# First MLP of a fused attention and two-MLP kernel: Strassen products in two token tiles where there were five, with another order of products and PSUM banks

## The chip, the cores and the metric

One core of one Trainium2 chip runs the kernel. The metric is device time of one execution in microseconds; a lower time is better. The profile is of one further execution of the same program.

## The reference, cut to what matters

```python
def reference(...):                       # 8 batches, 8 heads, 576 tokens, 64 per head
    q_s = softmax(q, axis=-1); k_s = softmax(k, axis=2)          # linear attention
    kv = einsum('bhsd,bhse->bhde', k_s, v)
    x = einsum('bhsd,bhde->bhse', q_s, kv) -> (4608 tokens, 512)
    xn = x / sqrt(mean(x * x) + 1e-6) * rms_g                    # first MLP, 512 -> 1536 -> 512
    x = (silu(xn @ w_gate) * (xn @ w_val)) @ w_out
    h = x @ w_in                                                 # second MLP, 512 -> 2048 -> 512
    return (h * sigmoid(1.702 * h)) @ w_out2
```

All results are float32; the weights arrive as float64, and the kernel decodes them into float32 on the chip.

## The kernel before

The 4608 tokens are cut into nine tiles of 512 (tile 0 to tile 8, `NTILE`). The first stage runs tile by tile: in tile j it computes the first MLP of tile j, and beside it the attention of tile j + 1 (four units of two heads each, nine steps a unit, `unit_steps`, L346), the norm of tile j + 1 (`norm_steps`, L483) and a share of the decoding of the second MLP's weights. Attention is finished in tile 6, since a batch has 576 tokens and its eighth batch covers tiles 7 and 8. Then the second stage computes the second MLP; the change does not touch it.

Every float32 product on TensorE is made of three passes of a rounded and a rest part (`PASSES`): high x high, high x rest, rest x high. So each operand needs a high half (a copy on ScalarE) and a low half (a subtraction on VectorE or GpSimd).

**Direct tiles** (0, 1, 2 and 8). The MLP's hidden dimension is cut into 12 blocks n. In three slots a block (36 slots a tile) TensorE makes the gate product of a block (`hidden`, 4 x 3 matmuls of 512 columns, PSUM tag "gv"), the value product, and then the output products of the block before (`out1_parts`, 12 matmuls into four "acc" banks). ScalarE takes silu of the gate, VectorE multiplies by the value (L1252) and splits the result in two halves (`split_u`). After the value product of the last block, the normalised tokens of the next tile are split into four "xs" rooms (`split_x`).

**Strassen tiles** (3 to 7, `by_strassen`, `FIRST, LAST = 3, NTILE - 2`). Two hidden blocks and both halves of the tokens and of the model dimension make a pair m, six pairs a tile. A pair takes seven products of quarter size in the order (1, 6, 2, 7, 5, 4, 3), each 2 x 2 x 3 matmuls of 256 columns, gate and value side by side in one bank. This is a step; a tile has 42 steps. Products 1, 6 and 5 open a bank of tag "gv", of which there are two; 2 adds to the bank of 1, 7 and 4 to that of 6, and 3 to that of 5. VectorE adds the banks to the partial sums (L870) and multiplies silu by value (L835, one step later than silu through the list `late`). After each product TensorE makes up to two output parts of the pair before (3 matmuls each, `PARTS`). Seven of a unit's nine attention steps write PSUM; attention has two banks of tag "att".

The left factors that are sums of weight blocks are made once (`prepare_steps`, L738: GpSimd adds, ScalarE and VectorE split, then stores to DRAM), twelve preparations spread over tiles 1 and 2. They are fetched again by DMA on SyncE's queue into a ring of six half rooms of gate and value weights (`fetch_sum`). The right factors, sums of token blocks, are made by `x_factor` (L790): GpSimd makes the sum (L798), ScalarE the high half, and VectorE or GpSimd the low half, one product at a time, in the last pair of the tile before, or after the last value product where the tile before is direct. Their rooms are four "xs" tiles and three pairs of weight rooms (`ASIDE`).

**What sets the order.** Each engine runs the instructions in the order in which the program lists them; the order is written by hand. `plan[j][slot]` holds the attention, norm and preparation steps of tile j; a Strassen tile maps its 36 slots onto its 42 steps (`plan_by_steps`). Attention steps of the tile behind a Strassen tile are put six slots earlier (`EARLIER`). `store_x2` (L629) empties an accumulator on ScalarE into one of two "ev" rooms and stores it by DMA from ScalarE's queue; in a Strassen tile the stores come as the last parts of the tile before are made, in steps 4, 5, 6 and 6.

PSUM has eight banks: "att" 2, "gv" 2, "acc" 4.

Of the kernel before, what the change touches and what calls it, by code (L numbers as in the profile page):

```python
# [20 lines left out]
def attention_glu_mlp(  # L21
# [58 lines left out]
    NPAIR = NF1 // 2  # L80
    FIRST, LAST = 3, NTILE - 2

# [7 lines left out]
    def f(x):  # L90
        return x.bitcast(F32)
# [241 lines left out]
    def load_v(u):  # L333
# [149 lines left out]
    def norm_steps(j):  # L483
# [59 lines left out]

        def spread():
            if j < 2:
                column_spread()
                return
            for i in range(1, T // P):
                invert(i)
            st["t"] = st["a"]  # L550
# [11 lines left out]

        return squares, total, spread, scale

# [151 lines left out]
    def pack_steps(kind, q):  # L716
# [8 lines left out]
    ITEMS = [  # L725
        (kind, m, p)
        for j in range(FIRST, LAST + 1)
        for m in range(NPAIR)
        for p in ORDER
        if LEFT[p] > 3  # L730
# [58 lines left out]

    def x_factor(j, p):  # L790
        block = [xr[j][:, k // 2 * 2 : k // 2 * 2 + 2, k % 2 * Q : (k % 2 + 1) * Q] for k in range(4)]
        if p in ORDER[:4]:
            w = x_room(8).rearrange("p e (c t) -> p e c t", c=2)
            xs[j, p] = [w[:, :, c] for c in range(2)]
        else:
            i = 2 * ORDER.index(p) - 8
            xs[j, p] = [room1(piece) for piece in ASIDE[i : i + 2]]
        put_op = lambda o, a, b, op: nc.gpsimd.tensor_tensor(o, a, b, op=op)  # L798
        if p in (6, 7, 4):
            x = ap.tile([P, T], F32, tag="sqa", bufs=1, name="xsum").rearrange(  # L800
                "p (c t) -> p c t", c=2
            )
            if p == 4:
                put_op(x, block[3], block[2], ALU.subtract)
                put_op(x, x, block[0], ALU.add)
            else:
                put_op(x, block[2], block[0], ALU.subtract)
                if p == 6:
                    put_op(x, x, block[1], ALU.add)
        elif p == 5:  # L810
            x = block[0]
            put_op(x, x, block[1], ALU.subtract)
        else:
            x = block[RIGHT[p]]
        side = nc.gpsimd if p in (1, 2, 3) else nc.vector
        if p in ORDER[:4]:
            halve(w[:, 0], w[:, 1], x, side)
        else:
            for c, w in enumerate(xs[j, p]):
                halve(w[:, 0], w[:, 1], x[:, c], side)  # L820

# [8 lines left out]
    def strassen_tile(j, plan, parts, aside):  # L830
# [14 lines left out]
        for m in range(NPAIR):  # L845
            d, h, s = {}, {}, {}
            rooms = pools["t"].tile([P, 2, 2, Q], F32, tag="xt", bufs=3, name="h")
            rooms = [rooms[:, 0], rooms[:, 1]]
            for k, p in enumerate(ORDER):
                if p in (1, 6, 5):  # L850
                    d[p] = bank("gv")
                t = d[{1: 1, 2: 1, 6: 6, 7: 6, 4: 6, 5: 5, 3: 5}[p]]
                for i, kind in enumerate("gv"):
                    w = left_factor(kind, m, p)
                    for c in range(2):
                        for n, (a, e) in enumerate(PASSES):
                            nc.tensor.matmul(  # L857
                                t[:, i * Q : (i + 1) * Q],
                                w[:, a, c * P : (c + 1) * P],
                                xs[j, p][c][:, e, :],  # L860
                                start=p in (1, 6, 5) and i == 0 and c == 0 and n == 0,
                                stop=c == 1 and n == 2,
                                skip_group_check=True,
                            )
# [5 lines left out]
                add = lambda o, a: nc.vector.tensor_tensor(o, a, both, op=ALU.add)  # L870
                if p == 1:
                    h["c1"] = rooms.pop(0)
                    nc.scalar.activation(h["c1"], both, AF.Copy)
                elif p == 6:
                    h["u2"] = rooms.pop(0)
                    add(h["u2"], h["c1"])
                elif p == 7:
                    h["u3"] = pools["t"].tile([P, 2, Q], F32, tag="xt", bufs=3, name="h3")
                    add(h["u3"], h["c1"])
                elif p == 2:  # L880
                    s[0] = sp.tile([P, T], F32, tag="s", bufs=2, name="s")
                    later.append(hidden_part(s[0], 1, both))
                else:
                    name, i, o = {5: ("u3", 1, 0), 4: ("c1", 1, 1), 3: ("u2", 0, 0)}[p]
                    add(h[name], h[name])
                    if p == 5:
                        s[1] = sp.tile([P, T], F32, tag="s", bufs=2, name="s")
                    later.append(hidden_part(s[i], o, h[name]))
                    if p != 5:
                        n, half = 2 * m + i, s[i]  # L890
                        later.append(lambda n=n, half=half: split_high(n, half))
                        later.append(
                            lambda n=n, half=half: late["now"].append(lambda: split_low(n, half))
                        )
# [12 lines left out]
                if k == 0 and m:  # L907
                    split_out_weight(2 * m - 2)
                if m == NPAIR - 1:
                    if by_strassen(j + 1):  # L910
                        x_factor(j + 1, p)
                    elif k < NC:
                        split_x(j + 1, k)
            for i in (1, 0):
                parts += out1_parts(j, 2 * m + i)
# [168 lines left out]
    with tc.manual_schedule():  # L1084
# [25 lines left out]
        steps = {u: unit_steps(u, "acc") for u in range(NC)}  # L1110
        squares, total, spread, scale = norm_steps(0)
        for _, u, s in ((x,abs(y),z) for x,y,z in sorted(first)):
# [42 lines left out]

        AT = (-1, 1, 2, 3, 4, 6, 7, 9, 10)
        EARLIER = 6

        for j in range(NTILE):
# [10 lines left out]
            if j + 1 < NTILE:  # L1170
                squares, total, spread, scale = norm_steps(j + 1)
                for c in range(NC):
# [15 lines left out]
        def plan_by_steps(j):  # L1188
            steps1 = [[] for _ in range(NPAIR * 7)]
            for slot in range(SLOTS):  # L1190
                steps1[slot * 7 // 6] += plan[j][slot]
            return lambda k: steps1[k]

# [9 lines left out]
        for j in range(NTILE):  # L1203
            if j == 1:
# [4 lines left out]
                depth.update(stage=1, w32=1)  # L1209
                fetch_next()  # L1210
            if by_strassen(j):
                strassen_tile(j, plan_by_steps(j), parts, aside)
                continue
# [24 lines left out]
            for slot in range(SLOTS):  # L1238
# [5 lines left out]
                elif part == 1:  # L1244
                    tv = hidden(j, weight["v", n])
                    if n == NF1 - 1 and by_strassen(j + 1):
                        for p in ORDER:
                            x_factor(j + 1, p)
# [255 lines left out]
```

## Time and profile before

| | |
|---|---|
| median of 3 runs | 1872.17 us (1871.8 to 1873.7) |
| profiled execution | 1870.15 us |
| its span (first to last instruction) | 1868.3 us |
| first stage, tiles 1 to 8 | 161.87 to 1153.31 us of the span |
| second MLP | 1153.31 us to the end |
| VectorE, ScalarE, GpSimd busy | 1275.2, 863.1, 567.6 us |

Times in the profile are microseconds from the start of the span. PE is TensorE's matmul stream and PEld its weight loads, which overlap it; DVE is VectorE, ACT ScalarE, POOL GpSimd, SP SyncE. A row of the timeline gives start, duration, engine, line, operation, what is written and read, how many were merged, and in brackets the idle time of the engine before it and what ended that. A releaser is inferred: of several things waited for, the last one is named. The clock is the share of TensorE's full speed that was granted.

### The profile page before, as it was taken

Reading aid. Unit: us, or ns where it says so; the run is one execution under the profiler, and the core shown is the slowest. Engines: PE = TensorE matmul, PEld = TensorE weight load, DVE = VectorE, ACT = ScalarE, POOL = GpSimd, SP = SyncE. Lnnn points to the kernel's source line nnn. Section 1 sums busy time; section 2 is a strip of 40 time slices with the busy share of each in tenths; the row PEclk is TensorE's granted clock in tenths of the full one; section 3 lists DMA queues with packets and bytes.
Section 4 is the critical chain, followed back from the end, with each engine's and each line's share of the span. In section 5 each row is a group of like instructions: output and inputs, shape, how many; then the busy total and the mean of one; then the engine's idle time right before and its main releaser. Section 6 shows DMA issues by size and latency. Waiting matters only on the chain.

```text
span 1868.3 us, 29842 instructions
## 1 busy us (share of the span) xinstructions
PE 1728.7 (93%) x11082; PEld 1557.6 (83%) x11082; DVE 1275.2 (68%) x2083; ACT 863.1 (46%) x1491; POOL 567.6 (30%) x506
## 2 busy tenths in 40 slices
PE   6999999968978978978989999999999999999998
PEld 4666777757867867867878888999999999999998
DVE  7997877867766656666645535655565788887776
ACT  6775454446445545444433334544444543333332
POOL 5875665562252242252231152311000510000000
PEclk9999999979989989989999999999999999999999
DMA  6664445446636635645444403455334573444442
GB/s 163 190 183 130 139 132 173 135 139 194 179 108 185 192 114 174 186 123 166 114 135 125 146 23 99 172 179 180 140 133 148 181 249 115 156 136 125 132 129 79
DMA packets 292129, 275.65 MB, mean 148 GB/s; under 512 B 63504, under 2 KB 273424, under 8 KB 291984
## 3 DMA queue, kind: packets, MB, share of 16 engines
q1 hardware_dynamic: 281856, 255.92, 44.8%
q10 hardware_dynamic: 10128, 17.83, 2.6%
q8 instruction: 87, 1.43, 0.3%
q14 instruction: 58, 0.48, 0.1%
HBM read 189.27 MB, written 84.41 MB: 146 GB/s over the span
## 4 chain that ended last, share of the span: by engine, by line
PE 66%; DVE 13%; ACT 8%; DMA 5%; POOL 4%; issue 4%; SPq 0%; ACTq 0%; DVEq 0%; POOLq 0%
PE ps_out L1416 19%; PE ps_in L960 19%; PE ps_gv L581 9%; PE ps_gv L857 8%; PE ps_acc L581 8%; DVE h L870 2%; DMA x<-ev 1%; ACT L396 1%; POOL xsum L798 1%; DVE sqa L542 1%; PE ps_acc L609 1%; DVE qs L402 1%; ACT ke L396 1%; DVE m L358 1%; DVE w L177 1%
## 5 line engine op out<-in xcount | busy, mean ns | idle before, releaser
L960 PE MATMUL ps_in<-xf,w2i 128*128 128x384 f32 x2016 | 350.3, 335 | 0.0
L960 PEld LDWEIGHTS ps_in<-xf,w2i 128*128 128x128 f32 x2016 | 349.9, 188 | 0.3 <-ACT h L972 0.2
L581 PE MATMUL ps_acc<-u,wo 128*128 128x512 f32 x1152 | 307.6, 399 | 0.8 <-ACT ev L637 0.4
L1416 PE MATMUL ps_out<-w2o,uf 128*128 128x256 f32 x2268 | 271.5, 281 | 0.0
L1416 PEld LDWEIGHTS ps_out<-w2o,uf 128*128 128x128 f32 x2268 | 269.6, 188 | 1.1
L186 POOL TENSOR_TENSOR wo<-raw,wo 128x512 fp32r<-128x512 f32 x96 | 130.3, 1358 | 435.1 <-ACT wo L185 369.7
L581 PEld LDWEIGHTS ps_acc<-u,wo 128*128 128x128 f32 x1152 | 205.7, 191 | 37.0 <-ACT ev L637 2.2
L857 PE MATMUL ps_gv<-xs,wg 128*128 128x256 f32 x720 | 119.4, 304 | 44.9 <-DVE h L870 28.4
L857 PEld LDWEIGHTS ps_gv<-xs,wg 128*128 128x128 f32 x720 | 104.8, 204 | 58.9 <-DVE h L870 36.2
L581 PE MATMUL ps_gv<-xs,wg 128*128 128x512 f32 x576 | 147.6, 404 | 4.5 <-DVE xs L573 3.8
L581 PE MATMUL ps_gv<-xs,wv 128*128 128x512 f32 x576 | 143.2, 396 | 1.2 <-POOL wv L186 1.2
L581 PEld LDWEIGHTS ps_gv<-xs,wg 128*128 128x128 f32 x576 | 107.9, 190 | 33.7 <-DVE xs L573 5.0
L870 DVE TENSOR_TENSOR h<-h,ps_gv 128x512 f32<-128x512 f32 x150 | 101.1, 674 | 48.7 <-PE ps_gv L857 45.4
L581 PEld LDWEIGHTS ps_gv<-xs,wv 128*128 128x128 f32 x576 | 106.5, 188 | 25.6 <-POOL wv L186 2.8
L945 ACT ACTIVATE h<-h 128x384 f32<-128x384 f32 x144 | 74.2, 525 | 112.1 <-DVE h L984 87.5
L657 DVE TENSOR_TENSOR raw<-raw 128x256 f32<-128x256 f32 (+1 forms) x236 | 106.6, 494 | 8.7 <-DMA raw<-w2d 6.7
L857 PE MATMUL ps_gv<-xs,wv 128*128 128x256 f32 x720 | 110.9, 292 | 0.0
L984 DVE TENSOR_TENSOR h<-h,ps_in 128x384 f32<-128x384 f32 x144 | 77.7, 552 | 47.7 <-PE ps_in L960 47.5
L834 ACT ACTIVATE s<-h 128x256 f32<-128x256 f32 x90 | 37.6, 418 | 141.8 <-DVE h L870 140.4
L1045 ACT ACTIVATE uf<-raw 128x1792 fp32r<-128x1792 f32 (+2 forms) x38 | 61.6, 1622 | 83.4 <-DVE raw L657 46.1
L857 PEld LDWEIGHTS ps_gv<-xs,wv 128*128 128x128 f32 x720 | 99.9, 200 | 0.0
L182 POOL TENSOR_TENSOR w<-w,stage 128x512 int32<-128x512 int32 x56 | 75.2, 1343 | 62.5 <-PE ps_gv L581 14.9
(202 smaller groups left out, 3018.6 us busy)
## 6 DMA issues: line engine op xcount, KB each, us to landing
u<-h SPq DMA_DIRECT2D x192, 192.0 KB, 1.9
wg<-w1s_g SPq DMA_DIRECT2D x120, 256.0 KB, 4.2
wv<-w1s_v SPq DMA_DIRECT2D x120, 256.0 KB, 4.4
stage<-in_moe_w_out_dram SPq DMA_DIRECT2D x28, 512.0 KB, 3.7
raw<-u SPq DMA_DIRECT2D x24, 512.0 KB, 4.5
x<-ev ACTq DMA_DIRECT2D x34, 256.0 KB, 2.9
stage<-in_moe_w_in_dram SPq DMA_DIRECT2D x16, 512.0 KB, 3.8
w2d<-w SPq DMA_DIRECT2D x32, 256.0 KB, 4.6
```

The costliest lines, as they stand in the source:

```text
L182: return scaled, signed, lambda: nc.gpsimd.tensor_tensor(dst, dst, lo, op=ALU.add)
L186: nc.gpsimd.tensor_tensor(dst[:, 1, :], src, f(dst[:, 0, :]), op=ALU.subtract)
L581: nc.tensor.matmul(t, w(a), x(e), start=first and i == 0, stop=last and i == 2)
L657: engine.tensor_tensor(raw[:, o], raw[:, a], raw[:, b], op=op)
L834: nc.scalar.activation(half, h[:, 0], AF.Silu)
L857: nc.tensor.matmul(t[:, i * Q : (i + 1) * Q], w[:, a, c * P : (c + 1) * P], xs[j, p][c][:, e, :], start=p in (1, 6, 5) and i == 0 and c == ...
L870: add = lambda o, a: nc.vector.tensor_tensor(o, a, both, op=ALU.add)
L945: nc.scalar.activation(dst, src, AF.Gelu_apprx_sigmoid)
L960: nc.tensor.matmul(t, w[:, a, s, c * P : (c + 1) * P], xfac[i, p, c][:, e, :], start=p in (1, 6, 5) and c == 0 and k == 0, stop=c == 1 and ...
L984: nc.vector.tensor_tensor(v, v, t, op=ALU.add)
L1045: nc.scalar.activation(ufac[k][:, 0, piece], uraw[k][:, 1:8][:, piece], AF.Copy)
L1416: nc.tensor.matmul(t[:, i * Q : (i + 1) * Q], u[:, a, LEFT[p] - 1, i * P : (i + 1) * P], w[:, e, m % 2, :], start=m == 0 and i == 0 and n ...
```

## The change

Only tiles 6 and 7 (the seventh and the eighth) go by Strassen; tiles 3, 4 and 5 go direct. In a Strassen tile the order of the products is (1, 6, 5, 2, 7, 4, 3), product 4 has a bank of its own, and products 1, 6, 5 and 4 go round three banks: two of tag "gv" and one, "third", that belongs to attention in the direct tiles. Attention has one bank there. After product 7 VectorE makes two additions, one of them with the bank of product 5. Attention and norm steps have a plan of their own in steps (`plan7`, `AT7`). The four stores of the tile before come in steps 4, 5, 7 and 8. The token sums are made by GpSimd in steps 33 to 36, the high halves from step 35 on, one a step, and the low halves one step later; in front of tile 6 the sums are made in slots 30 to 33, and two of the factors in slots 33 and 34. The twelve preparations are spread over tiles 1 to 4, three a tile, starting in slots 0, 8 and 16. Tile 5, the direct one ahead of a Strassen tile, has its attention and norm steps six slots earlier.

```diff
-    FIRST, LAST = 3, NTILE - 2
+    FIRST, LAST = 6, NTILE - 2
...
+    banks = {"att": ("att", "third"), "gv": ("gv", "gv"), "acc": ("acc",)}
+    turns = {"att": 0, "gv": 0, "acc": 0}
     def bank(tag):
-        bufs = {"att": 2, "gv": 2, "acc": 4}[tag]
+        tags = banks[tag]
+        turns[tag] += 1
+        tag = tags[(turns[tag] - 1) % len(tags)]
+        bufs = {"att": 1, "third": 1, "gv": 2, "acc": 4}[tag]
...
+    ORDER1 = (1, 6, 5, 2, 7, 4, 3)
...
+    def x_step(j, step):
+        for i, p in enumerate((6, 7, 5, 4)):
+            if step == 33 + i:
+                x_sum(j, p)
+        if step >= 35:
+            p = ORDER1[step - 35]
+            x_high(j, p)
+            side = nc.gpsimd if p in (1, 2, 3) else nc.vector
+            late["now"].append(lambda: x_low(j, p, side))
...
-            for k, p in enumerate(ORDER):
-                if p in (1, 6, 5):
+            for k, p in enumerate(ORDER1):
+                if p in (1, 6, 5, 4):
                     d[p] = bank("gv")
...
                 elif p == 7:
                     h["u3"] = pools["t"].tile([P, 2, Q], F32, tag="xt", bufs=3, name="h3")
                     add(h["u3"], h["c1"])
+                    add(h["c1"], h["u3"], d[5].rearrange("p (i f) -> p i f", i=2))
+                    s[1] = sp.tile([P, T], F32, tag="s", bufs=2, name="s")
+                    later.append(hidden_part(s[1], 0, h["c1"]))
...
-                else:
-                    name, i, o = {5: ("u3", 1, 0), 4: ("c1", 1, 1), 3: ("u2", 0, 0)}[p]
+                elif p in (4, 3):
+                    name, i, o = {4: ("u3", 1, 1), 3: ("u2", 0, 0)}[p]
...
-                        if m == 0 and len(parts) < NC:
-                            store_x2(j - 1, NC - 1 - len(parts))
+                for c in range(NC):
+                    if 7 * m + k == (4, 5, 7, 8)[c]:
+                        store_x2(j - 1, c)
...
+        AT7 = (0, 1, 3, 4, 6, 7, 9, 11, 12)
+        def divide_banks(strassen):
+            banks["gv"] = ("gv", "gv", "third") if strassen else ("gv", "gv")
+            banks["att"] = ("att",) if strassen else ("att", "third")
+            turns["gv"] = 0
...
+            if by_strassen(j):
+                for step, c, s in sorted(
+                    (AT7[s] + 7 * c - EARLIER, c, s) for c in range(len(mine)) for s in range(STEPS)
+                ):
+                    put7(j, step, steps[mine[c]][s])
...
-            ahead = EARLIER if by_strassen(j) else 0
+            ahead = EARLIER if by_strassen(j + 1) else 0
...
+            each = -(-len(preps) // (FIRST - 1))
             for i, steps1 in enumerate(preps):
-                j, slot = divmod(i * (FIRST - 1) * SLOTS // len(preps), SLOTS)
+                j, i = divmod(i, each)
                 for n, fn in enumerate(steps1):
-                    put(1 + j, slot + n, fn)
+                    put(1 + j, i * 24 // each + n, fn)
             for i in range(len(RING)):
-                put(FIRST - 1, 26 + i, fetch_sum)
+                put(FIRST - 1, 28 + i, fetch_sum)
+            for i, p in enumerate((6, 7, 5, 4)):
+                put(FIRST - 1, 30 + i, x_sum, FIRST, p)
+            def x_early(p):
+                x_high(FIRST, p)
+                x_low(FIRST, p, nc.gpsimd)
+            put(FIRST - 1, 33, x_early, 7)
+            put(FIRST - 1, 34, x_early, 4)
...
                     if n == NF1 - 1 and by_strassen(j + 1):
-                        for p in ORDER:
-                            x_factor(j + 1, p)
+                        for p in ORDER1[:4]:
+                            x_high(j + 1, p)
+                        for i, p in enumerate(ORDER1[:4]):
+                            x_low(j + 1, p, nc.vector if i < 2 else nc.gpsimd)
+                        x_high(j + 1, 3)
+                        x_low(j + 1, 3, nc.gpsimd)
```

`x_sum`, `x_high` and `x_low` are the three parts of the former `x_factor`: GpSimd's sum, ScalarE's copy into the room, and the subtraction on the engine named.

## Rows read from the trace of the kernel before

**Rows 1.** The page: busy time by engine, and the clock in 40 slices.
```profile
PE 1728.7 (93%) x11082; PEld 1557.6 (83%) x11082; DVE 1275.2 (68%) x2083; ACT 863.1 (46%) x1491; POOL 567.6 (30%) x506
PEclk9999999979989989989999999999999999999999
```

**Rows 2.** Busy time by stretch: length, engines with instructions, clock; tiles 1 to 8.
```profile
161.87:277.10 115.23, 112.86 (x565) 88.69 (x563) 86.59 (x129) 57.36 (x92) 67.31 (x54) 1.00 0.42 133
277.10:397.65 120.55, 114.68 (x590) 91.14 (x588) 97.62 (x144) 60.39 (x92) 68.06 (x54) 0.99 0.49 155
397.65:546.82 149.17, 110.57 (x772) 97.46 (x770) 96.10 (x169) 67.95 (x122) 58.31 (x45) 0.90 0.56 168
546.82:683.61 136.79, 112.27 (x783) 100.18 (x783) 89.16 (x157) 66.71 (x125) 46.43 (x36) 0.92 0.55 161
683.61:822.03 138.42, 114.15 (x782) 101.70 (x783) 89.20 (x157) 66.56 (x125) 46.10 (x36) 0.92 0.54 159
822.03:949.33 127.30, 110.87 (x761) 99.42 (x761) 78.53 (x136) 58.23 (x113) 38.20 (x30) 0.95 0.45 130
949.33:1048.27 98.94, 96.39 (x650) 88.06 (x651) 55.40 (x87) 38.49 (x77) 17.39 (x14) 0.98 0.46 134
1048.27:1153.31 105.04, 105.04 (x457) 85.56 (x456) 43.19 (x74) 31.43 (x71) 38.49 (x41) 1.00 0.21 67
```

**Rows 3.** Timeline of TensorE: stops at tile entries and inside Strassen tiles.
```profile
280.87 4.30 PE L581 MATMUL ps_gv<-xs,wg 128*128 128x512 f32 x11 [3.38 <-DVE xs L573]
...
397.65 0.28 PE L857 MATMUL ps_gv<-xs,wg 128*128 128x256 f32 x1
404.11 1.43 PE L857 MATMUL ps_gv<-xs,wg 128*128 128x256 f32 x5 [6.19 <-POOL xs L661]
...
417.11 1.62 PE L857 MATMUL ps_gv<-xs,wg 128*128 128x256 f32 x6 [9.85 <-ACT h L873]
...
531.29 1.01 PE L857 MATMUL ps_gv<-wg,wg 128*128 128x256 f32 x3 [6.69 <-DVE s L835]
...
715.69 0.48 PE L365 MATMUL ps_att<-ident,m 128*128 128x128 f32 x1 [5.52 <-DVE qL L455]
```

**Rows 4.** Timeline of ScalarE and VectorE at those stops.
```profile
406.68 0.63 ACT L660 ACTIVATE xs<-xsum 128x512 fp32r<-128x512 f32 x1 [9.29 <-POOL xsum L798]
...
416.32 0.68 DVE L1252 TENSOR_TENSOR s<-s,ps_gv 128x512 f32<-128x512 f32 x1
...
712.79 0.60 ACT L637 ACTIVATE ev<-ps_acc 128x512 f32<-128x512 f32 x1 [2.96 <-DMA x<-ev]
```

**Rows 5.** Busy time by stretch: the clock behind two stops.
```profile
281.81:285.22 3.41, 3.41 (x10) 2.62 (x9) 3.34 (x6) 0.01 (x1) 0.00 (x0) 0.50 0.77 270
...
527.57:534.40 6.83, 3.11 (x13) 3.06 (x14) 3.56 (x7) 4.07 (x6) 2.52 (x3) 0.50 0.52 170
```

**Rows 6.** Line 554's instructions: duration in ns; and its four ahead of tile 2.
```profile
L554 DVE SCALAR_TENSOR_TENSOR xr<-xr,g_sb,sqa x28: 734/745/1806, 273.2 to 1027.1; 128x512 f32<-128x512 f32 x28
...
273.22 5.86 DVE L554 SCALAR_TENSOR_TENSOR xr<-xr,g_sb,sqa 128x512 f32<-128x512 f32 x4
```

**Rows 7.** Timeline of products 7 and 5, in tile 5 and in tile 7.
```profile
696.60 0.63 PE L857 MATMUL ps_gv<-wg,wg 128*128 128x256 f32 x3 [0.46 <-DVE s L835]
...
990.27 1.56 PE L581 MATMUL ps_acc<-u,wo 128*128 128x512 f32 x6
990.47 0.69 DVE L870 TENSOR_TENSOR h<-h,ps_gv 128x512 f32<-128x512 f32 x1 [2.12 <-PE ps_gv L857]
991.08 0.41 DVE L835 TENSOR_TENSOR s<-s,ps_gv 128x256 f32<-128x256 f32 x1
991.67 0.52 PE L857 MATMUL ps_gv<-wg,wg 128*128 128x256 f32 x3
```

**Rows 8.** Timeline of TensorE: first products of two pairs of tile 7.
```profile
983.20 0.86 PE L857 MATMUL ps_gv<-xs,wg 128*128 128x256 f32 x6
...
998.74 0.86 PE L857 MATMUL ps_gv<-xs,wg 128*128 128x256 f32 x6
```

More of the change, by code (lines that the diff above doesn't have):

```diff
@@ L542, in invert, with spread @@
             nc.vector.reciprocal(out=a, in_=a)
-        def spread():
+        def spread(inverts=True):
             if j < 2:
@@ L547, in spread @@
                 return
-            for i in range(1, T // P):
+            for i in range(1, T // P if inverts else 0):
                 invert(i)
@@ L561, in scale @@
             )
-        return squares, total, spread, scale
+        return squares, total, spread, scale, invert
     def x_room(o):
@@ L728, in attention_glu_mlp @@
         for m in range(NPAIR)
-        for p in ORDER
+        for p in ORDER1
         if LEFT[p] > 3
@@ L788, in left_factor, with x_blocks, x_sum @@
         return weight[kind, n][:, :, o * Q : (o + 1) * Q]
[L790 to L794, printed above, removed]
-        else:
[L796 to L800, printed above, removed]
+    xsum = {}
+    def x_blocks(j):
+        return [xr[j][:, k // 2 * 2 : k // 2 * 2 + 2, k % 2 * Q : (k % 2 + 1) * Q] for k in range(4)]
+    def x_sum(j, p):
+        b = x_blocks(j)
+        put_op = lambda o, a, b, op: nc.gpsimd.tensor_tensor(o, a, b, op=op)
+        if p == 5:
+            x = b[0]
+            put_op(x, x, b[1], ALU.subtract)
+        else:
+            pool, tag, bufs = (ap, "sqa", 1) if p == 6 else (sp, "ev", 2)
+            x = pool.tile([P, T], F32, tag=tag, bufs=bufs, name="xsum").rearrange(
                 "p (c t) -> p c t", c=2
@@ L803, in x_factor, with x_source, x_high, x_low @@
             if p == 4:
-                put_op(x, block[3], block[2], ALU.subtract)
-                put_op(x, x, block[0], ALU.add)
+                put_op(x, b[3], b[2], ALU.subtract)
+                put_op(x, x, b[0], ALU.add)
             else:
-                put_op(x, block[2], block[0], ALU.subtract)
+                put_op(x, b[2], b[0], ALU.subtract)
                 if p == 6:
[L809 to L812, printed above, removed]
-        else:
[L814 to L817, printed above, removed]
-        else:
-            for c, w in enumerate(xs[j, p]):
-                halve(w[:, 0], w[:, 1], x[:, c], side)
+                    put_op(x, x, b[1], ALU.add)
+        xsum[j, p] = x
+    def x_source(j, p):
+        return xsum[j, p] if p in (4, 5, 6, 7) else x_blocks(j)[RIGHT[p]]
+    def x_high(j, p):
+        x = x_source(j, p)
+        if p in ORDER1[:4]:
+            w = x_room(8).rearrange("p e (c t) -> p e c t", c=2)
+            nc.scalar.activation(w[:, 0], x, AF.Copy)
+            xs[j, p] = [w[:, :, c] for c in range(2)], w
+        else:
+            i = 2 * ORDER1.index(p) - 8
+            rooms = [room1(piece) for piece in ASIDE[i : i + 2]]
+            for c, w in enumerate(rooms):
+                nc.scalar.activation(w[:, 0], x[:, c], AF.Copy)
+            xs[j, p] = rooms, None
+    def x_low(j, p, side):
+        x = x_source(j, p)
+        rooms, w = xs[j, p]
+        if w is not None:
+            side.tensor_tensor(w[:, 1], x, f(w[:, 0]), op=ALU.subtract)
+        else:
+            for c, w in enumerate(rooms):
+                side.tensor_tensor(w[:, 1], x[:, c], f(w[:, 0]), op=ALU.subtract)
+    def x_step(j, step):
[7 more added lines that the diff above has]
+            late["now"].append(lambda: x_low(j, p, side))
     PARTS = (0, 1, 1, 2, 1, 1, 2)
@@ L859, in strassen_tile @@
                                 w[:, a, c * P : (c + 1) * P],
-                                xs[j, p][c][:, e, :],
-                                start=p in (1, 6, 5) and i == 0 and c == 0 and n == 0,
+                                xs[j, p][0][c][:, e, :],
+                                start=p in (1, 6, 5, 4) and i == 0 and c == 0 and n == 0,
                                 stop=c == 1 and n == 2,
@@ L882, in strassen_tile @@
                     later.append(hidden_part(s[0], 1, both))
-                else:
-                    name, i, o = {5: ("u3", 1, 0), 4: ("c1", 1, 1), 3: ("u2", 0, 0)}[p]
+                elif p in (4, 3):
+                    name, i, o = {4: ("u3", 1, 1), 3: ("u2", 0, 0)}[p]
                     add(h[name], h[name])
-                    if p == 5:
-                        s[1] = sp.tile([P, T], F32, tag="s", bufs=2, name="s")
                     later.append(hidden_part(s[i], o, h[name]))
[L889 to L894, printed above, removed]
+                    n, half = 2 * m + i, s[i]
+                    later.append(lambda n=n, half=half: split_high(n, half))
+                    later.append(
+                        lambda n=n, half=half: late["now"].append(lambda: split_low(n, half))
+                    )
                 run_late()
@@ L909, in strassen_tile @@
                 if m == NPAIR - 1:
-                    if by_strassen(j + 1):
-                        x_factor(j + 1, p)
-                    elif k < NC:
+                    if not by_strassen(j + 1) and k < NC:
                         split_x(j + 1, k)
+                if by_strassen(j + 1):
+                    x_step(j + 1, 7 * m + k)
             for i in (1, 0):
@@ L1156, in attention_glu_mlp, with put7 @@
         AT = (-1, 1, 2, 3, 4, 6, 7, 9, 10)
+        AT7 = (0, 1, 3, 4, 6, 7, 9, 11, 12)
         EARLIER = 6
+        NSTEP = 7 * NPAIR
+        plan7 = [[[] for _ in range(NSTEP)] for _ in range(NTILE)]
+        def divide_banks(strassen):
+            banks["gv"] = ("gv", "gv", "third") if strassen else ("gv", "gv")
+            banks["att"] = ("att",) if strassen else ("att", "third")
+            turns["gv"] = 0
+        def put7(j, step, fn, *args):
+            if step >= 0:
+                plan7[j][step].append(lambda: fn(*args))
+            elif by_strassen(j - 1):
+                plan7[j - 1][NSTEP + step].append(lambda: fn(*args))
+            else:
+                put(j - 1, SLOTS + step * 6 // 7, fn, *args)
         for j in range(NTILE):
@@ L1162, in attention_glu_mlp @@
                 steps[u] = unit_steps(u)
-            ahead = EARLIER if by_strassen(j) else 0
+            if by_strassen(j):
[3 more added lines that the diff above has]
+                    put7(j, step, steps[mine[c]][s])
+                squares, total, spread, scale, invert = norm_steps(j + 1)
+                for c in range(NC):
+                    put7(j, AT7[-1] + 7 * c - EARLIER, squares, c)
+                put7(j, 35 - EARLIER, total)
+                for i in (1, 2, 3):
+                    put7(j, 35 + (i + 1) // 2 - EARLIER, invert, i)
+                put7(j, 36 - EARLIER, spread, False)
+                for c in range(NC):
+                    put7(j, 37 + c // 2 - EARLIER, scale, c)
+                continue
+            ahead = EARLIER if by_strassen(j + 1) else 0
             order = sorted((AT[s] + 6 * c - ahead, c, s) for c in range(len(mine)) for s in range(STEPS))
@@ L1210, in attention_glu_mlp @@
                 fetch_next()
+            divide_banks(by_strassen(j))
             if by_strassen(j):
-                strassen_tile(j, plan_by_steps(j), parts, aside)
+                strassen_tile(j, lambda k, j=j: plan7[j][k], parts, aside)
                 continue
```

14 lines of the change are left out of this document (4 added, 10 removed).

## The prediction

> **What bounds the kernel now.** I read the page first: TensorE is busy 93% of the span, so TensorE's stream, its waits and its clock set the time [rows 1]. Then I cut the span into the nine tiles of the first stage (each window runs from the start of a tile's first gate/value product to that of the next) and read one line per tile [rows 2]. The reader is to see three kinds of tile. Tiles 1 and 2 work directly and carry attention beside them: 115.23 and 120.55 us, TensorE busy nearly throughout. Tiles 3 to 6 work by Strassen and carry attention too: 149.17, 136.79, 138.42 and 127.30 us, although TensorE is busy there for only 110.57 to 114.15 us, and part of that at a lower mean clock (0.90 to 0.95). Tiles 7 and 8 carry no attention: Strassen 98.94, direct 105.04. So Strassen gains 6 us where nothing disturbs it, and loses some 20 us where attention shares the engines. What is lost is idle time and clock, not products.
>
> The instructions in order of time show where TensorE stops. Entering tile 3 it waits 6.19 us and then 9.85 us; later 6.69 us for a bank, and in tile 5 5.52 us for an attention bank [rows 3]. The other engines at these moments tell why: ScalarE stood 9.29 us for a token sum that GpSimd had not made, VectorE came to the product that frees a bank (L1252) only at 416.32, behind all the low halves of those sums, and ScalarE stood 2.96 us for a store to land before it could empty the next accumulator [rows 4]. After each long stop the clock falls: the 6.83 us around 531 run at 0.50 of full speed, the 1.2 GHz level, and so do 3.41 us at the entry of tile 2, after a gap of 3.38 us [rows 3, 5].
>
> **The change, part by part.**
> *Tiles 3, 4, 5 go direct.* Of the trace, tiles 1 and 2 are the same work: 288 + 144 products of 512 columns, attention for one tile, the same decodes. Tile 2 without its entry is 120.55 - 3.38 (gap) - 1.7 (half of the 3.41 us at half clock) = 115.5 [rows 2, 3, 5]; tile 1, which has no such entry, is 115.23. I take 115.4 plus an entry.
> *The entry from direct to direct.* In front of tile 2 VectorE scales the four token blocks in 5.86 us, though one such instruction has a median of 0.745 us: four alone would be 3.0 [rows 6]. GpSimd is then making weight sums. These move: 12 preparations stood in tiles 1 and 2 up to their last slots; they now stand in tiles 1 to 4, three a tile, from slots 0, 8 and 16, so none is at a tile's end. That takes up to 2.9 us from a gap of 3.38; GpSimd still decodes and splits output weights there. Bounds per entry: 0, and 5.1 as now (3.38 + 1.7). I take 1.5, nearer to the lower, for tiles 2, 3, 4. For tile 5 the attention for tile 6 starts six slots early, at the end of tile 4, as it does now at the end of tile 2, where the wait was 6.19: bounds 0 and 7.9 (6.19 + 1.7), I take 4.
> The Trainium skill (SBUF — State Buffer, "Who interferes with whom") says that a VectorE instruction with two SBUF inputs is shut out while GpSimd reads SBUF. The stretched scales agree with it; by it alone every entry would be 0 once the preparations are gone, some 8 us less in all than I count. I do not go by it because other GpSimd work stays.
> *Tile 6 becomes the first Strassen tile.* Its TensorE work at full clock is 110.87 - 0.05 x 127.30 = 104.5 us [rows 2]. Entry: the sums on GpSimd are made from slot 30 on, the scaling is six slots earlier, and L1252 now waits behind two low halves on VectorE, not behind all. So the 9.85 goes, and of the 6.19 I leave 2 (bounds 0 and 16.0, the whole old entry). If GpSimd is late with a sum again, ScalarE holds up everything queued behind the high half that waits for it, as in the 9.29 [rows 4].
> *Stores apart.* The four evictions move from steps 4, 5, 6, 6 to 4, 5, 7, 8, so the third no longer meets the first one's transfer. That ends the 5.52 us stop and the clock loss behind it; accumulator 3 is wanted again at step 10, two steps after its store. Sums one pair ahead (GpSimd at steps 33 to 36, ScalarE from 35, low halves a step later) end the 6.69 us stop in pair 5. All this is in the 104.5, which has no idle time. The sums pass GpSimd's output-weight splits, which are wanted a pair later; nothing waits.
> *Third bank, and what takes its place.* The new order is 1, 6, 5, 2, 7, 4, 3; banks go round in threes, so product 4 opens the bank in which 1 and 2 were summed. That bank is free when VectorE has made s x bank, which stands behind the two additions that follow product 7. Today the same product stands behind one addition, and TensorE has two output parts meanwhile. From the rows of tile 7: product 7 ends at 990.27, the addition starts at 990.47, the product 0.61 later, lasts 0.41, and TensorE goes on 0.18 behind its end, at 991.67, when its six output products are just over [rows 7]. New: 0.20 + 0.61 + 0.61 + 0.41 + 0.18 = 2.01 us, with one output part of 0.70 as cover (half of 990.27 to 991.67): a wait of 1.3 us in every pair. Queued behind product 4 are its output parts and product 3. With attention the old chain already costs 0.46 [rows 7], so 1.8 there. Six pairs: 10.6 us in tile 6, 7.8 in tile 7. Bounds: 0, if attention's own products fill the hole, and twice as much.
> *One attention bank in tile 6.* 26 of the 28 attention steps that write PSUM fall in tile 6 and hand one bank on, one a step of 15.54 / 7 = 2.2 us [rows 8]. Bounds: 0, because most evictions are shorter than a step, and 26 x 5.52. The nearest row is the 0.46: a third of the steps waiting so makes 4.
> *Tile 7*: 96.39 - 0.02 x 98.94 = 94.4 at full clock; six pairs of 15.54 are 93.2, which agrees [rows 2, 8]. Plus 7.8, plus 1.2 for the norm's share of VectorE: 103.4.
> *The rest at nothing.* Ring fetches start two slots later, and are out before the tile ends; were the cover gone, one landing of some 4 us would stand in tile 6's entry. Fewer sums are fetched; no wait above names them. Tile 8 and the second MLP are not touched.
>
> Sum: tile 1 115.2 (0); tiles 2, 3, 4 at 116.9 (-3.7, -32.3, -19.9); tile 5 119.4 (-19.0); tile 6 104.5 + 2 + 10.6 + 4 = 121.1 (-6.2); tile 7 (+4.5). Together -76.6. The profiled execution took 1870.15 us, 1.85 more than its span, and becomes 1793.5; the median of the runs is 2.0 above it, so 1795.5.
>
> **The rivals.**
> *Lighter.* The new waits are filled (attention's products fall into the hole, tile 7 hides its norm) and entries vanish: tile 6 106.5, tile 7 95.5, entries 7 less. 29.5 below: 1766. For it: VectorE is busy only 55.40 of 98.94 us in tile 7 [rows 2]. Against it: the chain behind product 7 is one of order, not of load.
> *Heavier.* Direct tiles 2 to 5 keep the old entry (120.55 each, +12.2) and the single attention bank makes tile 6 as long as the old tile 5, 138.42 (+17.3): 1825. For it: decodes and splits still stand beside the scaling. Against: no preparation does.
> *The clock falls in the new Strassen tiles.* If each pair's wait brings the clock to 1.2 GHz for 6.83 us [rows 5], 3.4 us go each time: 12 x 3.4 = 41, 1836.5. For it: short waits now come in every pair, with attention's beside them. Against it: the only rows of a fall stand behind waits of 3.38 us and more. The Trainium skill (TensorE: Matmul & The Clock Gate, "A second HAM failure mode: psum-queue depth-cycling") tells of a kernel whose small waits at bank changes made the clock go up and down; by that rule this rival comes true.
> *Slower.* One attention bank turns each of 26 hand-overs in tile 6 into a stop like the 5.52 us one, because ScalarE or VectorE is always several instructions behind: 143.5 us, 1939. It decides against the change from 76.6 / 26 = 2.9 us a hand-over. Against it: a step gives 2.2 us of cover, and the 5.52 came from a store that now stands apart.
>
> **How the numbers follow.** Forecast 0.61 (its own range 1781 to 1810), lighter 0.15, heavier 0.15, clock 0.06, slower 0.03. The 8-in-10 range takes half of lighter and half of heavier: 1775 to 1818. A measurement here tells 0.2% from no change; 76.6 us is 4%, and only the last rival ends above: faster 0.96, within 0.2% 0.01, slower 0.03.
>
> **What would show it.** Right: tiles 3 to 5 at 115 to 120 us each with TensorE busy all but 2 to 5 us; in tiles 6 and 7 a wait of about 1.3 us (1.8 with attention) in front of every product 4, put down to VectorE's L835; tile 7 longer than before, 102 to 105; no stop over 3 us inside tile 6 and no half clock there; L1252 no longer among its releasers. Wrong: a direct tile above 122 us, tile 7 below 98 (the wait is filled), or many small attention-bank waits summing to over 10 us in tile 6.

## The result, and the profile after

Median 1792.53 us (1789.25 to 1792.79) against 1872.93: a ratio of 0.9565, 95% interval 0.9548 to 0.9581. The profiled execution has a span of 1791.0 us. Forecast: 1795.5, range 1775 to 1818.

The stretches of the first stage, as in [rows 2]: length, then TensorE, its weight loads, VectorE, ScalarE and GpSimd busy with their instructions, clock, DMA share, GB/s; tiles 1 to 8, and four short stretches of tile 6.

```profile
162.11:276.31 114.20, 112.34 (x564) 88.96 (x563) 78.70 (x128) 54.83 (x90) 44.66 (x36) 1.00 0.37 115
276.31:390.99 114.68, 111.52 (x567) 89.54 (x566) 84.50 (x136) 55.20 (x87) 44.84 (x37) 1.00 0.37 116
390.99:505.35 114.36, 111.51 (x567) 89.38 (x566) 84.53 (x136) 55.20 (x87) 44.89 (x37) 1.00 0.38 117
505.35:621.39 116.04, 112.75 (x589) 90.20 (x588) 86.87 (x140) 57.45 (x93) 43.26 (x36) 1.00 0.35 112
621.39:736.79 115.40, 112.14 (x548) 91.05 (x547) 80.96 (x136) 52.88 (x92) 32.11 (x24) 0.97 0.31 94
736.79:869.24 132.45, 110.36 (x770) 99.22 (x768) 78.28 (x143) 60.12 (x114) 47.23 (x38) 0.94 0.46 135
869.24:970.66 101.42, 95.38 (x651) 86.72 (x650) 49.83 (x84) 37.10 (x73) 17.86 (x14) 1.00 0.45 135
970.66:1075.99 105.33, 105.31 (x457) 85.47 (x456) 43.27 (x74) 31.43 (x71) 38.27 (x41) 1.00 0.21 66
743.52:750.35 6.83, 4.16 (x18) 3.97 (x19) 2.77 (x5) 2.86 (x4) 3.98 (x6) 0.50 0.36 114
...
767.41:770.82 3.41, 3.41 (x30) 3.29 (x27) 1.89 (x8) 2.77 (x6) 0.64 (x1) 0.50 0.82 235
...
791.31:794.72 3.41, 3.41 (x31) 3.29 (x30) 2.91 (x9) 1.94 (x4) 0.13 (x1) 0.50 0.66 193
815.20:818.61 3.41, 3.41 (x30) 3.29 (x31) 2.77 (x9) 2.08 (x4) 0.00 (x0) 0.50 0.00 0
```

Against [rows 2], tiles 3, 4 and 5 gave 34.8, 20.8 and 23.0 us, tile 2 5.9 and tile 1 1.0; tiles 6 and 7 took 5.2 and 2.5 more. Tile by tile against the prediction: direct tiles 0.9 to 4.0 us lighter, 10.6 together; tile 6 11.3 heavier (121.1 foreseen); tile 7 2.0 lighter. The errors cancel, and that the total came within 3 us is luck: its parts did not.

What TensorE waited for in tile 6 (line waited for: us, times, longest):

```profile
PE ps_att L417 <- ACT xr L478: 9.9, 3, 4.6
PE ps_att L447 <- POOL qe L411: 4.6, 1, 4.6
PE ps_third L893 <- DVE s L871: 2.3, 2, 1.1
PE ps_gv L893 <- DVE s L871: 1.8, 1, 1.8
PE ps_gv L893 <- ACT s L870: 1.1, 1, 1.1
```

The largest is the single attention bank. The timeline shows why ScalarE came so late to empty it (L478), before the first products of the next unit (L417):

```profile
760.45 1.28 ACT L402 ACT_TABLE_LOAD   x1
761.74 0.74 ACT L402 ACTIVATE ke<-k_sb 128x640 f32<-128x640 f32 x1
762.39 0.72 ACT L402 ACTIVATE qe<-q_sb 128x640 f32<-128x640 f32 x1
763.12 1.28 ACT L870 ACT_TABLE_LOAD   x1
764.99 0.42 ACT L870 ACTIVATE s<-h 128x256 f32<-128x256 f32 x1 [0.59 <-DVE h L906]
766.16 0.63 ACT L875 ACTIVATE u<-s 128x512 fp32r<-128x512 f32 x1 [0.75 <-DVE s L871]
766.69 0.36 ACT L478 ACTIVATE xr<-ps_att 128x256 f32<-128x256 f32 x1
...
767.11 1.12 PE L417 MATMUL ps_att<-v_sb,ke 128*64 128x65 f32 x20 [4.61 <-ACT xr L478]
```

The next unit's exponentials, with two loads of tables around them, and the silu and split behind them stand in ScalarE's order ahead of a 0.36 us copy.

### The profile page after: what moved, and what is told of

Its sections match the earlier page's. It is cut to its first block, busy times and chain, and to the rows that moved or that the text cites. A ratio compares the mean times of both kernels' runs of the same rounds, so it can differ in the third digit from the quotient of the medians.

```text
span 1791.0 us, 27957 instructions
## 1 busy us (share of the span) xinstructions
PE 1722.0 (96%) x10434; PEld 1525.8 (85%) x10434; DVE 1227.2 (69%) x2007; ACT 820.0 (46%) x1383; POOL 500.7 (28%) x456
## 4 chain that ended last, share of the span: by engine, by line
PE 77%; DVE 12%; ACT 6%; issue 1%; DMA 1%; SPq 1%; POOL 1%; ACTq 0%; DVEq 0%; POOLq 0%
PE ps_out L1494 20%; PE ps_in L997 20%; PE ps_gv L587 18%; PE ps_acc L587 11%; PE ps_gv L893 3%; PE ps_third L893 2%; DVE xr L560 2%; ACT L402 1%; DVE sqa L548 1%; PE ps_acc L615 1%; DVE h L906 1%; DVE m L364 1%; ACT ke L402 1%; DVE qs L408 1%; DVE qe L411 1%
## 5 line engine op out<-in xcount | busy, mean ns | idle before, releaser
L587 PE MATMUL ps_gv<-xs,wg 128*128 128x512 f32 x1008 | 255.5, 401 | 6.5 <-DVE xs L579 6.2
L587 PE MATMUL ps_gv<-xs,wv 128*128 128x512 f32 x1008 | 250.5, 396 | 1.5 <-POOL wv L186 1.5
L587 PEld LDWEIGHTS ps_gv<-xs,wg 128*128 128x128 f32 x1008 | 188.7, 190 | 55.2 <-DVE xs L579 8.1
L587 PEld LDWEIGHTS ps_gv<-xs,wv 128*128 128x128 f32 x1008 | 185.9, 188 | 43.0 <-POOL wv L186 3.0
L1317 ACT ACTIVATE s<-ps_gv 128x512 f32<-128x512 f32 x84 | 50.2, 597 | 240.1 <-PE ps_gv L587 240.0
L1330 DVE TENSOR_TENSOR s<-s,ps_gv 128x512 f32<-128x512 f32 x84 | 57.0, 678 | 99.8 <-PE ps_gv L587 89.4
L1494 PE MATMUL ps_out<-w2oq,uf 128*128 128x256 f32 x756 | 90.9, 281 | 0.0
L1494 PEld LDWEIGHTS ps_out<-w2oq,uf 128*128 128x128 f32 x756 | 90.1, 188 | 0.0
L1086 DVE TENSOR_TENSOR uf<-raw,uf 128x1792 fp32r<-128x1792 f32 (+2 forms) x38 | 72.9, 1924 | 18.1 <-ACT uf L1082 18.1
L408 DVE TENSOR_REDUCE qs<-qe 128x10 f32<-128x640 f32 x32 | 26.2, 819 | 78.4 <-ACT qe L402 78.3
```

Source lines behind the costliest of these rows:

```text
L587: nc.tensor.matmul(t, w(a), x(e), start=first and i == 0, stop=last and i == 2)
L1086: nc.vector.tensor_tensor(w[:, 1, piece], raw[:, piece], f(w[:, 0, piece]), op=ALU.subtract)
L1330: nc.vector.tensor_tensor(s, s, tv, op=ALU.mult)
L1494: nc.tensor.matmul(t[:, i * Q : (i + 1) * Q], u[:, a, LEFT[p] - 1, i * P : (i + 1) * P], w[:, e, m % 2, :], start=m == 0 and i == 0 and n ...
```

## The experiments

Times are medians; intervals are of the ratio to the kernel before.

**Which half of the change gives the gain.** One run keeps the old Strassen schedule and changes the number of tiles, with the preparations spread as the change spreads them:

```diff
-    FIRST, LAST = 3, NTILE - 2          # kernel before
+    FIRST, LAST = 6, NTILE - 2
-                j, slot = divmod(i * (FIRST - 1) * SLOTS // len(preps), SLOTS)
+                j, i = divmod(i, 3)
-                    put(1 + j, slot + n, fn)
+                    put(1 + j, i * 8 + n, fn)
```

> The kernel of before with only the number of Strassen tiles changed to two (tiles 6 and 7) and the twelve preparations spread over tiles 1 to 4; order of products, banks, stores, token sums and attention slots inside a Strassen tile as before. Theory A (the gain comes from the three tiles that leave Strassen): tile 6 is then the entry tile of the old schedule, about 149 us as tile 3 was, against 132.5 in the changed kernel, tile 7 98.9 against 101.4: 1792.5 + 16.7 - 2.5 = about 1807 us. Theory B (the gain comes from the new schedule inside the Strassen tiles): most of the 80 us is gone, 1840 us or more.

The other keeps five tiles and changes the schedule (`FIRST = 3` in the changed kernel).

> The changed kernel with five Strassen tiles again (3 to 7), so that only the new schedule is left of the change. Theory A: a Strassen tile that carries attention keeps costing more than a direct one, some 127 to 132 us against 115: about 1792.5 + 40 - 5 = 1827 us. Theory B: each Strassen tile gains 6 us on a direct one, 1792.5 - 18 = about 1775 us.

Measured: 1789.32 us (0.9559, 0.9545 to 0.9573) and 1858.32 (0.9926, 0.9911 to 0.9941). The number of tiles, with the preparations spread, gives the whole gain; theory B falls. The first came 18 us below what theory A foresaw: the old schedule's entry tile takes 136.63 us here and not 149, and tile 5 111.5 and not 115.4. The second came 31 us above theory A: its Strassen tiles 3 to 5 take 132.9 to 134.3 us, 17 to 20 more than the direct ones of the change, and tiles 1 and 2 carry six preparations each again and take 120.02 and 122.47 us, 5.8 and 7.8 more. To see whether the new schedule is worth anything at two tiles, both were timed side by side:

> The changed kernel itself, beside the next run on the same chip: 1790 to 1793 us.

> The kernel of before with two Strassen tiles and the preparations spread, as once before. Theory A (the new schedule inside the Strassen tiles is worth nothing at two tiles: it saves some 4 us in tile 6 and loses as much at its entry and in tile 7): the same as the run beside it within 0.2%, or up to 4 us less. Rival (the new schedule gains): 1800 us or more.

1791.89 (0.9574, 0.9561 to 0.9588) for the change and 1789.98 (0.9561, 0.9548 to 0.9574) for the old schedule: the intervals overlap, and the difference is 0.1%. Tiles 5, 6 and 7 of the old schedule in two tiles:

```profile
620.24:731.75 111.51, 111.51 (x590) 90.28 (x588) 78.43 (x138) 53.54 (x89) 23.70 (x18) 1.00 0.33 99
731.75:868.65 136.90, 108.78 (x750) 96.93 (x748) 82.58 (x144) 59.62 (x114) 49.25 (x39) 0.91 0.44 130
868.65:967.91 99.26, 97.22 (x650) 89.17 (x651) 54.98 (x87) 38.49 (x77) 17.36 (x14) 0.97 0.44 134
```

The new schedule saves 4.8 us in tile 6 (136.90 to 132.07 in the run beside it) and pays 1.2 in tile 4 (116.06 against 114.86), 2.8 in tile 5 (114.30, where attention starts early) and 2.2 in tile 7 (101.45). So at two tiles it gains nothing. At five tiles it was worth 13 us, 0.7%.

**What Strassen is worth at all.** Two runs of the changed kernel with fewer Strassen tiles:

```diff
-    FIRST, LAST = 6, NTILE - 2
+    FIRST, LAST = 8, 7                  # none; the other run: FIRST = 7
-            if j == LAST + 1:
+            if FIRST <= LAST and j == LAST + 1:
```

> The changed kernel with no Strassen tile in the first stage (no weight sums, no ring). Theory A: tile 6 costs 115.4 instead of 132.5, tile 7 105.3 instead of 101.4: about 1779 us, faster than the change. Theory B: slower than the change by 6 us a tile, about 1804 us.

> The changed kernel with Strassen in tile 7 alone, which carries no attention; preparations over six tiles, two a tile. Theory A: tile 6 about 115.5 us instead of 132.5, tile 7 about 103 with an entry: about 1777 us, the fastest. Theory B: one Strassen tile less, about 1798 us.

All direct: 1745.54 us (0.9326, 0.9312 to 0.934). One Strassen tile: 1767.0 (0.9439, 0.9424 to 0.9455). Theory A has the direction, and misses the size by 33 and 10 us. All direct is the fastest kernel found, 47 us below the change. Its tiles 1, 2, 5, 6 and 7:

```profile
161.37:272.58 111.21, 111.21 (x564) 89.12 (x563) 71.36 (x126) 52.01 (x88) 24.16 (x18) 1.00 0.28 82
272.58:382.98 110.40, 110.40 (x568) 89.82 (x566) 76.10 (x133) 52.11 (x85) 24.13 (x18) 1.00 0.28 85
...
603.75:714.06 110.31, 110.31 (x567) 89.62 (x566) 76.08 (x133) 52.36 (x89) 24.15 (x18) 1.00 0.29 85
714.06:824.43 110.37, 110.37 (x567) 89.82 (x566) 73.02 (x128) 48.02 (x81) 18.20 (x14) 1.00 0.16 47
824.43:924.51 100.08, 100.08 (x435) 81.44 (x434) 33.79 (x53) 23.92 (x40) 15.52 (x12) 1.00 0.03 11
```

TensorE never stops in them: busy time is the whole length. And without preparations a direct tile with attention is 110.4 us, where I had taken 115.4 for its own cost. So the preparations themselves seem to cost TensorE's path 4 us a tile: three a tile 114.4 to 114.7 (tiles 2 and 3), two a tile (one Strassen tile) 113.18. In tile 2 of the change TensorE waits mainly at three places where all direct shows no wait, each time for VectorE:

```profile
277.68 2.83 PE L587 MATMUL ps_gv<-xs,wg 128*128 128x512 f32 x11 [0.98 <-DVE xs L579]
...
322.46 0.33 PE L371 MATMUL ps_third<-ident,m 128*128 128x128 f32 x1 [0.88 <-DVE qL L461]
...
342.87 0.33 PE L371 MATMUL ps_att<-ident,m 128*128 128x128 f32 x1 [1.05 <-DVE qL L461]
```

**What a preparation costs with.** Into the kernel with all tiles direct I put the preparations back, first without halves and stores, then without stores alone (nothing reads their results):

```diff
+        for i, (m, kind) in enumerate((m, kind) for m in range(NPAIR) for kind in "gv"):
+            j, i = divmod(i, 3)
+            for n, fn in enumerate(prepare_steps(kind, m)[:3]):   # the other run: all four steps
+                put(1 + j, i * 8 + n, fn)
...
-            nc.sync.dma_start(out=w1s_d[kind, m][:, :, 0], in_=f(z))    # the other run only, 3 stores
```

> All tiles direct, and beside them the twelve preparations where the changed kernel has them (three in each of tiles 1 to 4), but of each only GpSimd's additions: no split into halves, no stores; nothing reads the sums. Tiles 2 to 4 took 110.4 us without any preparation and 114.4 in the changed kernel with all of it. Theory A (GpSimd's additions stretch VectorE's two-input instructions, and TensorE waits for these): most of the 4 us is back, 113 us a tile and more, with the 1 us wait at the tile's entry; in all about 1757 us. Rival (the halves do it, standing on ScalarE and VectorE ahead of what TensorE waits for): 111 us a tile, no entry wait, 1747 us.

> As the run before, with the halves made too, only the stores to DRAM left out. Theory A: 114 us a tile, hardly more than with the additions alone; about 1760 us. Rival (halves): 114 us, where the additions alone gave 111. If both stay near 111, the stores' traffic is the cost.

1754.25 us (0.937, 0.9357 to 0.9382) and 1760.99 (0.9407, 0.9394 to 0.942). Tile 2 of each:

```profile
274.44:387.20 112.76, 110.75 (x567) 89.72 (x566) 80.88 (x133) 52.11 (x84) 43.91 (x37) 1.00 0.29 83
```

```profile
275.88:390.55 114.67, 111.50 (x568) 89.53 (x566) 84.44 (x136) 55.05 (x87) 44.87 (x37) 1.00 0.28 82
```

GpSimd's additions cost 2.4 of the 4.3 us of this tile (112.76 - 110.40); with them VectorE's same 133 instructions take 80.88 us instead of 76.10. The halves cost 1.9 more, the stores nothing (114.67 against 114.68 in the change). Theory A gets its half and the entry wait (0.97 us, as in the change), the rival the other half. All preparations together: 1760.99 - 1745.54 = 15.5 us.

**The waits inside the Strassen tiles.** Three edits of the changed kernel for the three waits, and one that undoes the stores:

```diff
# e5, attention results of tile 6 emptied by VectorE
-  nc.scalar.activation(xraw(j, c)[:, o : o + n], t[:, done : done + n], AF.Copy)
+  nc.vector.tensor_copy(xraw(j, c)[:, o : o + n], t[:, done : done + n])
# e6, unit 28's query block scaled by VectorE
-  side = nc.gpsimd if u < 2 * NC or u >= (FIRST + 1) * NC else nc.vector
+  side = nc.gpsimd if u < 2 * NC or u > (FIRST + 1) * NC else nc.vector
# e7, one output part from behind product 2 to behind product 7
-  PARTS = (0, 1, 1, 2, 1, 1, 2)
+  PARTS = (0, 1, 1, 1, 2, 1, 2)
# e9, stores as before
-  if 7 * m + k == (4, 5, 7, 8)[c]:
+  if 7 * m + k == (4, 5, 6, 6)[c]:
```

> The changed kernel; in tile 6 alone VectorE instead of ScalarE empties the attention results out of PSUM. Theory A (the stops of 4.61, 2.63 and 2.63 us in front of an attention unit's first products come from the single attention bank being emptied by ScalarE behind the next unit's exponentials): they go, and the half clock behind each: tile 6 from 132.5 to about 119 us, in all about 1780 us. Rival (one bank is too few, whoever empties it): the waits stay, put down to VectorE, and tile 6 stays above 129 us.

1788.38 us (0.9555, 0.9541 to 0.9569); tile 6 128.23, so neither forecast of its length comes true. Theory A falls in its reason. TensorE still waits before the same products, and VectorE's order shows the same thing as ScalarE's did: its copy (L479) stands behind the sum that waits 3.29 us for the exponentials.

```profile
762.02 0.82 DVE L408 TENSOR_REDUCE qs<-qe 128x10 f32<-128x640 f32 x1 [3.29 <-ACT qe L402]
...
764.93 0.41 DVE L479 COPY xr<-ps_att 128x256 f32<-128x256 f32 x1
...
765.44 0.80 PE L417 MATMUL ps_att<-v_sb,ke 128*64 128x65 f32 x20 [4.18 <-issue]
```

So the longest of the three stops seems to come from the place of the last eviction, behind the next unit's exponentials, whichever engine makes it. The profile names no releaser here; the copy ends at 765.34, 0.1 us before TensorE goes on. An order with the eviction ahead, which would show it, was not run. The other two such stops shrank from 2.63 to 1.59 us, and no half clock stands behind them.

> The changed kernel; VectorE instead of GpSimd scales the query block of the one attention unit at tile 6's entry. Theory A (the 4.55 us stop there is GpSimd's queue: token sums and low halves stand ahead of that scaling): the stop and the 6.83 us of half clock behind it go, 6 to 8 us: about 1785 us. Rival (the low halves of the third product's tokens on the same queue, over at 743.5 us, hold TensorE next): the stop shrinks to 2 us and the clock still falls, 1790 us.

1791.54 us (0.9571, 0.9556 to 0.9585): the median hardly moved, which fits the rival's time, but not its reason. The stop shrank from 4.55 to 3.14 us, now put down to VectorE's evictions of the same bank (L434) and not to GpSimd's low halves, and behind it the profile shows the full clock:

```profile
743.80:750.00 6.20, 5.90 (x40) 5.19 (x41) 4.29 (x7) 3.22 (x5) 3.23 (x4) 1.00 0.32 80
...
743.85 0.52 PE L447 MATMUL ps_att<-ident,qe 128*128 128x128 f32 x3 [3.14 <-DVE kvL L434]
```

Tile 6 is 128.90 us in this profile, which is of the fastest of the four executions (1788.87, the others up to 1793.26). In this run VectorE makes the scaling itself (1.60 us) ahead of those evictions, so it does not tell how long the stop would be without either.

> The changed kernel with one output part (three products, 0.7 us) moved from behind product 2 to behind product 7. Theory A (product 4 waits for a bank that VectorE frees behind two additions): the waits of 1.14 to 1.77 us in four of six pairs of tile 7 shrink by 0.7 each, tile 7 from 101.4 to 98.6 us, tile 6 by 2 to 3: about 1787 us. Rival (TensorE then waits as long in front of product 7 or in the next pair): no change, 1792 us.

1787.34 us (0.9553, 0.9537 to 0.9569). The profile decides this one: tile 7 is 98.71 us (98.6 expected), and the wait in its second pair fell from 1.14 to

```profile
891.87 0.50 PE L893 MATMUL ps_gv<-wg,wg 128*128 128x256 f32 x2 [0.45 <-DVE s L871]
```

which is 0.69 less, the length of the part moved. Three of the four waits of tile 7 shrank so, and the chain behind product 7 is shown for them. The wait in the fifth pair did not (1.77 us, now 1.81): there VectorE comes to the two additions only at 940.73, behind 4.8 us of reciprocals and scalings for the norm (L548, L560).

> The changed kernel with the four stores of a Strassen tile back in steps 4, 5, 6 and 6. Theory A (the third eviction meets the first one's transfer and holds ScalarE, and the attention bank behind it): a stop near 5.5 us and half clock behind it in tile 6, 6 to 12 us: about 1801 us. Rival (with the new order of steps ScalarE is not waited for at that place): no change, 1792 us.

1794.82 us (0.959, 0.9576 to 0.9605); tile 6 134.67. The stop in front of the second unit grew from 4.61 to 6.6 us, the other stops stayed within 0.1 us: the stores apart are worth some 2 us in one tile, less than theory A's 6.

## Why the prediction was right, point by point

- *Tiles 3 to 5 go direct*: right, and all of the gain (the old schedule in two tiles has it too). The size of a direct tile, 115.4, was right for the wrong reason: tiles 1 and 2 of before both carry preparations, 4 to 5 us of their length, which I priced at an entry wait only. All direct shows 110.4. Spreading did not remove the cost, it shared it out: tiles 1 and 2 of before are 4.0 and 10.2 us longer than with all tiles direct, 14 together, and the preparations in tiles 1 to 4 cost 15.5.
- *Entries between direct tiles*: I took 1.5; TensorE waited 0.96 to 0.98. GpSimd runs ahead of the others, so a preparation written into slot 0 still meets the scaling at the end of the tile before: the four of tile 1's end take 5.90 us, much as in [rows 6], and 4.84 with all tiles direct.
- *Entry of tile 5*: 4 taken; the wait is 3.26 and half clock stands behind it, but the tile has 548 instructions of TensorE against 567, those moved ahead into tile 4.
- *Product 4's wait*: the mechanism and the price hold in tile 7. There (VectorE and TensorE, two pairs):

```profile
895.18 0.69 DVE L906 TENSOR_TENSOR h<-h,ps_third 128x512 f32<-128x512 f32 x1 [5.71 <-PE ps_third L893]
895.90 0.69 DVE L906 TENSOR_TENSOR h<-h,ps_gv 128x512 f32<-128x512 f32 x1
896.50 0.41 DVE L871 TENSOR_TENSOR s<-s,ps_gv 128x256 f32<-128x256 f32 x1
...
896.98 0.62 PE L893 MATMUL ps_gv<-wg,wg 128*128 128x256 f32 x3 [1.14 <-DVE s L871]
```

```profile
879.32 0.69 DVE L906 TENSOR_TENSOR h<-h,ps_gv 128x512 f32<-128x512 f32 x1 [5.13 <-PE ps_gv L893]
880.04 0.69 DVE L906 TENSOR_TENSOR h<-h,ps_third 128x512 f32<-128x512 f32 x1
880.06 0.61 PE L893 MATMUL ps_gv<-wg,wg 128*128 128x256 f32 x3
880.65 0.41 DVE L871 TENSOR_TENSOR s<-s,ps_gv 128x256 f32<-128x256 f32 x1
```

  Two additions and the product, 1.14 us against 1.3 foreseen. But pairs 0 and 3 start product 4 when the first addition ends, before the product of s and the bank (880.65): there it was given the other bank. So it is four pairs of six, and tile 7 is 101.4 instead of 103.4. In tile 6 the waits in front of product 4 come to 5.8 us, where 10.6 was taken: the longest beside attention is 1.12 us, not 1.8.
- *One attention bank*: the term that was mis-sized. I took 4 us from a wait of 0.46; three stops alone are 9.9, each followed by half clock, because an eviction waits for more than the step before it. The sum has no term for that clock in tile 6: its four stretches at 0.50 hold 4.16 and three times 3.41 us of TensorE's work, and half of it, some 7 us by an estimate from these rows, is what the clock cost. The bound of 0 "because most evictions are shorter than a step" looked at the eviction, not at what stands ahead of it.
- *Entry of tile 6*: no wait at the first products, as foreseen to 2 us, but 4.55 behind the second, put down to the queue of GpSimd, where the low halves of the token factors stand ahead; 3.14 of it were left when GpSimd no longer made that scaling. In the change the clock falls behind it.
- *Stores apart*: the 5.52 us stop is gone, but the attention bank's 4.61 stands in the same pair; with the stores back in the old steps that one is 2 us longer, and this is what they are worth.
- *"Strassen gains 6 us where nothing disturbs it"*: wrong. Tile 8's 105.04 holds 24 output products more than a direct tile in mid-row (456 products against 432, 5.5 us): twelve because a Strassen tile leaves two blocks over instead of one, and twelve because the last tile finishes its own. The fair figure is 100.08, so Strassen gained 1.1 us in tile 7 before, and loses 1.3 in the change, not counting its preparations. TensorE's own work is 4.7 us less (95.38 busy against 100.08); the waits take it back.
- *The rivals*: in the change no half clock stands behind product 4's waits of 1.14 to 1.78 us (tile 7 has clock 1.00), so the clock rival does not come true there; behind the attention bank's stops of 2.63 us and more the clock fell. The rule of the Trainium skill named with that rival (TensorE: Matmul & The Clock Gate, "A second HAM failure mode: psum-queue depth-cycling") is not borne out by these waits. The rival is not dead: with five Strassen tiles half clock stood behind three waits in front of product 4 of 2.84 to 2.85 us and one of 1.77. "Heavier" was right of tile 6, "lighter" of the direct tiles.
- *The signs*: two that were to show the prediction right did not come. There are stops over 3 us inside tile 6 (4.55 and 4.61) with half clock behind them, and product 4 waits in four pairs of tile 7, not six. Tile 3 (114.36) and tile 7 (101.42) lie just below their ranges. And the attention bank's waits in tile 6, 9.9 us and 0.4 more (L470), reach the 10 us that were to show it wrong, as three long stops and not as many small ones. So the account of tile 6 was wrong, though the time was right.

## What to carry to other kernels

Price a fast algorithm by the whole stage: in the tile without attention fewer products on TensorE were here worth 1 to 2 us (98.94 before and 98.16 in the old schedule at two tiles, against 100.08 direct), while the sums that feed them cost 15.5 us in all, and the Strassen tile beside attention took 22 us more than a direct one (132.45 against 110.37), by its stops and the clock behind them. With tile 5 (5 us), tile 7 (1.3) and the 12 output products that tile 6 leaves to tile 8 (3) this makes the 47 us between the change and all direct. A baseline tile that carries work for the scheme under study hides the scheme's cost; look for, or run, one that does not. Where one buffer is handed round, look at what stands ahead of the eviction on its engine, not at how long the eviction is.

## What the runs showed of the hardware

Stops of 2.63 us were enough for half clock: the stretch from 791.31 to 794.72 of the first fence (granted 0.50) stands behind

```profile
791.15 1.14 PE L417 MATMUL ps_att<-v_sb,ke 128*64 128x65 f32 x18 [2.63 <-ACT xr L478]
```

The rows shown [rows 3, 5] have falls only behind 3.38 us and more, but the kernel before had one behind 2.24 us, in its tile 6:

```profile
782.38 0.62 PE L857 MATMUL ps_gv<-wg,wg 128*128 128x256 f32 x3 [2.24 <-DVE s L835]
...
783.57:786.98 3.41, 3.41 (x16) 3.12 (x15) 2.00 (x4) 0.94 (x2) 0.30 (x1) 0.50 0.88 263
```

In the run with the output part moved, half clock stood once behind a wait of 1.77 us in tile 6; behind a wait of 1.81 us in tile 7 it did not. In the run with five Strassen tiles it stood behind a wait of only 1.23 us, in front of an attention product of tile 4 (544.91, granted 0.50 from 545.27 to 548.68). And the 3.14 us stop of the run with the scaling on VectorE was followed by none. So a stop under 3 us is no safe side, the length of the stop alone does not decide, and which ones are followed by a fall is not settled here.
